# One of the two upper-half shuffles of the last but one pair of inverse outputs issued from SyncE's queue

## Chip, core and metric

The kernel runs on one core of one Trainium2 chip. The time is device microseconds of one execution, and the number that counts is the median of several executions. TensorE (PE) multiplies matrices, VectorE (DVE), ScalarE (ACT) and GpSimd (POOL) do the rest of the arithmetic, and SyncE (SP) computes nothing: it issues DMA transfers. GpSimd and ScalarE can issue transfers too.

## The reference

One layer of an H3-like state-space mixer is followed by a token-mixing MLP, in bf16, with S = 2048 positions and D = 448 channels:

```
h_q  = layernorm(x)                                  # x = A_q, over channels
kv   = shift_conv(k, shift_k, 4 taps) * v
y    = irfft(rfft(pad(kv)) * rfft(pad(ssm_k)))[:S]   # long causal convolution, per channel
h    = x + h_q * (y + kv * ssm_D)
u    = gelu(einsum("bsd,sf->bdf", layernorm(layernorm(h)), w1) + b1)     # F = 1792
out  = h + transpose(einsum("bdf,fs->bds", u, w2) + b2)
```

## The kernel before

The position axis is split as 128 partitions times R = 16 rows. The Fourier transforms are done as two matrix stages with a shuffle between them: `k1`, `k2` for the filter, `u1`, `u2` for `kv`, and back with `i1` and `i2`. A shuffle is a set of DMA transfers from SBUF to SBUF, since the second stage needs another index on the partitions than the first one leaves there.

The inverse transform is the place of the change. `emit_products_i1` (L1147 on) runs over eight pairs jj = 0 to 7. For each pair VectorE forms the products of the two spectra (L1161), TensorE multiplies them by the inverse tables (L1178), ScalarE evicts two PSUM pairs into the tile `TU` (the eviction helper, L739), and the two outputs j = 2jj and j = 2jj + 1 are then shuffled from `TU` into `TZ`. In every pair but jj = 7 each j has an upper transfer of 112 partitions (196 KB, issued by GpSimd) and a lower one of 16 partitions (28 KB, issued by SyncE), all at L1201. The upper transfer fills rows r = 0 to 13 of `TZ`, the lower one rows 14 and 15. The pair jj = 7 is done otherwise: its four transfers of 98 KB (L1190; three from SyncE, one from ScalarE) fill rows 2 to 15, and for rows 0 and 1 TensorE reads `TU` itself through small tables `EW`, which four small transfers of 4 KB (L1128, SyncE) prepare.

`emit_i2` then does the second inverse stage row by row. For r = 0 and 1 TensorE runs two matmuls on `TZ` (L1300) and four on `TU` (L1308); for the other rows only L1300. VectorE combines the result with the normalised input (L1337 for r = 0 to 3; for r from 4 on ScalarE or VectorE gates it first, L1317 or L1319, then L1327), takes statistics (L1343, L1346, with GpSimd's L1379 for the power) and writes the normalised row `Q` (L1386). The first MLP product (L1433) reads `Q` row by row; L1443 is its second half of columns, and L1455 the second MLP product, with L1458 adding the residual. All weights of the first product are loaded in four pieces (L1406; the second to fourth wait for the L1190 transfers), the rest later (L1410, L1417).

Each engine's order of work is written out by hand in `ORDER`, as tokens `step:operations`. The pair jj = 1, with j = 2 and 3, is the last but one that is worked on: TensorE takes the pairs as jj = 0, 6, 3, 4, 5, 2, 1, 7. Its step is `i1.4`: operations 18 and 20 are the upper transfers of j = 2 and 3, 19 and 21 the lower ones. `ct0.1:2-5` are the four L1128 transfers, `i1.6:22` a lower transfer of another pair, and `i1.16:22`, `i1.16:20`, `i1.16:19` the three L1190 transfers of SyncE. TensorE's order in `i2` is r = 0, 1, 4, 2, 7, 3, 6, 5, 8 and on; VectorE combines r = 0, 1, 2, 3 in this order.

A first pass in the program replays these orders with estimated costs, which fixes PSUM buffers and semaphores; the chip runs each engine's queue in the written order.

Of the kernel before, what the change touches and what calls it, by code (L numbers as in the profile page):

```python
# [78 lines left out]
    ),  # L79
# [8 lines left out]
    ),  # L88
}

# [493 lines left out]
def _build(nc, A_q, A_k, A_v, A_shift_k, A_ssm_k, A_ssm_D, B_w1, B_b1, B_w2, B_b2, out):  # L584
# [11 lines left out]
    DB = 2 * D  # L596
# [23 lines left out]
    o_TU = 104064  # L620
    o_KN = o_TU
    o_W2 = (o_TK, o_TU)
    o_TZ = 132736
# [15 lines left out]
    with ctx:  # L639
# [58 lines left out]
        def MR(s):  # L698
            return view(o_WR + s * 4 * DB, [4, D])
# [13 lines left out]
        def Pb(b, i=0):  # L713
            return PS[:, b.slots[i], 0:D]

        def Ppair(b):
            s0, s1 = b.slots
            return PS[:, s0:s1 + 1, 0:D]
# [15 lines left out]
        def evac(dst, src, w, b, n, scale=None, engs=FX, r=(), est=None):  # L734

            def fn(e, W):
                if W == "act":
                    if scale is None:
                        return e.copy(out=dst(), in_=src())  # L739
                    return e.activation(out=dst(), in_=src(), func=ACT.Copy, scale=scale)  # L740
                if scale is None:
                    return e.tensor_copy(out=dst(), in_=src())
                return e.tensor_scalar(out=dst(), in0=src(), scalar1=scale, scalar2=None, op0=ALU.mult)
            bs = [b] if b is not None else []
            return op(engs, fn, r=r, w=w, br=bs, n=n, kind="psum", est=est)
# [405 lines left out]
        def emit_products_i1():  # L1151
            for jj in range(R // 2):
                ms = []
                for h in range(2):
                    i = 2 * jj + h
                    sch.t0 = T_I1 + T_DI1 * i
                    m = _Buf(mring)
                    ms.append(m)
                    ru = (o_TU + i * 2 * DB, 2 * DB)
                    aft = [x for w in wbufs for x in w.readers] if i == 0 else [mfirst[0]]  # L1160
                    op("dve", lambda e, W, m=m, i=i: e.tensor_tensor(  # L1161
                        out=MR(m.slots[0]).rearrange("p (x y) d -> p x y d", x=2),
                        in0=TU[:, i].unsqueeze(2).broadcast_to([128, 2, 2, D]),
                        in1=TK[:, i].unsqueeze(1).broadcast_to([128, 2, 2, D]), op=ALU.mult),
                       r=[ru, (o_TK + i * 2 * DB, 2 * DB)], bw=[m], n=4 * D, after=aft)
                    if i == 0:
                        mfirst.append(len(sch.ops) - 1)
                bs = [_Buf(psum, 2) for _ in range(2)]
                if jj == 1:
                    sch.tag = "ct0"  # L1170
                    emit_ct(False)
                    sch.tag = "i1"
                mt = (MA, MB, MN) if jj < R // 2 - 1 else ML
                for h in range(2):
                    for t, (tab, xy) in enumerate(((mt[0], 0), (mt[2], 3), (mt[1], 1), (mt[1], 2))):
                        for par in range(2):
                            P = slice(64 * par, 64 * par + 64)
                            k = op("pe", lambda e, W, b=bs[h], m=ms[h], par=par, t=t, tab=tab, xy=xy, P=P: e.matmul(  # L1178
                                Pb(b, par), tab[P, :], MR(m.slots[0])[P, xy, :], start=(t == 0), stop=(t == 3)),
                               r=r_iv if jj < R // 2 - 1 else [(o_ML, 768)], br=[ms[h]], bw=[bs[h]], n=D, est=94.5, mode=3)  # L1180
                            i1_last.append(k)
                    evac(lambda jj=jj, h=h: TU[:, 2 * jj:2 * jj + 2, h, :], lambda b=bs[h]: Ppair(b),
                         [(o_TU + (4 * jj + h) * DB, DB), (o_TU + (4 * jj + 2 + h) * DB, DB)], bs[h], 2 * D)
                if jj == R // 2 - 1:
                    for h in range(2):
                        for par in range(2):
                            j = 2 * jj + par
                            p0 = 64 * (j & 1) + 32 * ((j >> 1) & 1) + (j >> 2)
                            o_h = o_TU + (2 * j + h) * DB
                            k = op("act" if h and par == 0 else "sp", lambda e, W, j=j, h=h, p0=p0: e.dma_start(  # L1190
                                TZ[p0:p0 + 29:4, NZ:R, h, :], TU[0:8 * (R - NZ), j, h, :]),
                                   r=[(o_h, DB)], w=[(o_TZ + NZ * 2 * DB, (14 - NZ) * 2 * DB, "zpool"), (o_TZ + 28 * DB, 4 * DB, "zsp")],
                                   dmab=8 * (R - NZ) * DB, keng=8)
                            shuf["zpool"] = k
                            shuf.setdefault("zl", []).append(k)
                    continue
                for par in range(2):
                    j = 2 * jj + par
                    p0 = 64 * (j & 1) + 32 * ((j >> 1) & 1) + (j >> 2)
                    for q_, a, b_, j0 in (("pool", 0, 112, 0), ("sp", 112, 128, 14)):  # L1200
                        shuf["z" + q_ + str(j)] = shuf["z" + q_] = op(q_, lambda e, W, j=j, p0=p0, a=a, b_=b_, j0=j0: e.dma_start(  # L1201
                            TZ[p0:p0 + 29:4, j0:j0 + (b_ - a) // 8].rearrange("p r c d -> p r (c d)"),
                            TU[a:b_, j].rearrange("p c d -> p (c d)")),
                           r=[(o_TU + j * 2 * DB, 2 * DB)], w=[(o_TZ + j0 * 2 * DB, (b_ - a) // 8 * 2 * DB, "z" + q_)],
                           dmab=(b_ - a) * 2 * DB, keng=8)

        def emit_warm(n_, t0):
# [219 lines left out]
        def emit_mlp():  # L1427
# [21 lines left out]
            for r in range(R):  # L1449
# [24 lines left out]
                ("u1", emit_stage1, (V, o_V, TU, o_TU, "u")),    # L1474
                ("xload", emit_xload, ()), ("bias", emit_bias, ()), ("q", emit_q, ()),
                ("u2", emit_stage2, (TU, o_TU, None)), ("ew", emit_ew, ()), ("i1", emit_products_i1, ()), ("ct", emit_ct, (True,)), ("xn", emit_xn, ()), ("w1a", emit_w1_load, (0,)),
                ("warm", emit_warm, (N_WZ, T_I2 - 50.0)),
                ("i2", emit_i2, ()), ("w1b", emit_w1_load, (1,)), ("w2", emit_w2_load, ()), ("mlp", emit_mlp, ()))
# [39 lines left out]
```

## Time and profile before

| what | value |
|---|---|
| median of 3 executions | 173.56 us (173.31 to 173.61) |
| the profiled execution | 173.39 us, its span 171.5 us |
| busy: PE, DVE, ACT, POOL | 162.2, 101.5, 92.6, 59.7 us |
| granted TensorE clock | full in all 40 slices |
| chain that ended last | PE 68%, ACT 18%, DMA 8%, DVE 3% |
| upper transfers of L1201 | 14 from GpSimd, 196 KB each, median 4.2 us from issue to landing |

Times in the views are us from the start of the span. The span leaves out 1.9 us of the execution's own time. A timeline row gives start, length, engine, line, operation and how many were merged, and in brackets the idle time before them with what ended it. A row of the chain gives start, length and what the end of the program was waiting for in that stretch. DMA-issuing instructions are shown on the queue of the engine that issues them (SPq is SyncE's, ACTq ScalarE's), with the time that the issue took, which is not the time of the transfer.

### The profile page before, as it was taken

What the parts mean: (1) busy time and instruction counts of PE and PEld (TensorE: products, weight loads), DVE (VectorE), ACT (ScalarE), POOL (GpSimd) and SP (SyncE); (2) the same over time, 40 slices, a digit from 0 to 9 for tenths busy, and PEclk for the clock granted to TensorE, in tenths of its full rate; (3) what the DMA queues carried; (4) which work ended last, traced back from release to release, by engine and by line L of the source; (5) the groups of instructions that cost most, each with busy time, mean ns of one, the idle gap of its engine ahead of it and who ended that gap; (6) DMA issues with size and microseconds to landing.
All of it is one profiled execution on the core that took longest, in us unless ns stands there. A gap on an engine that the chain in (4) does not pass through costs nothing.

```text
span 171.5 us, 3572 instructions
## 1 busy us (share of the span) xinstructions
PE 162.2 (95%) x1425; PEld 95.0 (55%) x1425; DVE 101.5 (59%) x188; ACT 92.6 (54%) x132; POOL 59.7 (35%) x152
## 2 busy tenths in 40 slices
PE   6999999889889999968999999999999999999994
PEld 2776745443334433543455555555567777777783
DVE  7997988869999999979999830000003133132231
ACT  3699688988999999969866536321210000000000
POOL 8344837581810686445887830000000000000000
PEclk9999999999999999999999999999999999999999
DMA  5999587584959756646899999990000111101111
GB/s 161 417 321 378 182 264 285 211 325 162 286 145 369 268 162 204 177 147 222 278 320 380 411 424 414 420 396 30 0 0 4 53 53 53 53 0 57 53 53 54
DMA packets 15628, 35.15 MB, mean 205 GB/s; under 512 B 3740, under 2 KB 9740, under 8 KB 15612
## 3 DMA queue, kind: packets, MB, share of 16 engines
q1 hardware_dynamic: 12468, 28.25, 45.5%
q0 software_dynamic: 2880, 6.49, 11.9%
q8 instruction: 11, 0.18, 0.4%
q10 hardware_dynamic: 264, 0.18, 0.3%
q14 instruction: 5, 0.04, 0.1%
HBM read 22.05 MB, written 1.84 MB: 139 GB/s over the span
## 4 chain that ended last, share of the span: by engine, by line
PE 68%; ACT 18%; DMA 8%; DVE 3%; issue 1%; POOL 1%; SPq 0%; DVEq 0%
PE ps L1455 25%; PE ps L1433 12%; PE ps L1443 12%; ACT arena L739 9%; DMA arena<-arena 8%; ACT arena L1070 5%; PE ps L1095 5%; PE ps L1178 4%; ACT arena L848 2%; PE ps L1060 2%; PE ps L1026 2%; PE ps L1300 2%; ACT arena L740 2%; PE ps L993 1%; DVE arena L1337 1%
## 5 line engine op out<-in xcount | busy, mean ns | idle before, releaser
L1458 DVE SCALAR_TENSOR_TENSOR arena<-ps,arena 128x448 bf16<-128x448 f32 (+2 forms) x17 | 11.1, 656 | 56.9 <-PE ps L1455 56.9
L1455 PE MATMUL ps<-arena 128*128 128x448 bf16 (+2 forms) x238 | 42.7, 342 | 0.0
L1455 PEld LDWEIGHTS ps<-arena 128*128 128x128 bf16 x238 | 33.3, 145 | 9.5
L739 ACT CAST arena<-ps 128x896 bf16<-128x896 f32 x30 | 24.6, 1012 | 0.2 <-PE ps L1095 0.2
L1433 PE MATMUL ps<-arena 128*128 128x448 bf16 x112 | 22.5, 353 | 0.7 <-DVE arena L1375 0.7
L1070 ACT CAST arena<-ps 128x896 bf16<-128x896 f32 x24 | 20.5, 919 | 3.2 <-PE ps L1060 3.2
L1076 POOL DMA_DIRECT2D arena<-arena x32 | 17.6, 556 | 11.8 <-ACT arena L1070 9.7
L1443 PE MATMUL ps<-arena 128*128 128x448 bf16 x112 | 21.4, 352 | 0.0
L1423 ACT ACTIVATE arena<-ps,arena 128x448 bf16<-128x448 f32 x14 | 8.3, 635 | 18.9 <-PE ps L1443 14.6
L1095 PE MATMUL ps<-arena 128*64 128x448 bf16 x128 | 15.2, 359 | 2.3 <-ACT arena L739 0.8
L1433 PEld LDWEIGHTS ps<-arena 128*128 128x128 bf16 x112 | 10.7, 98 | 11.4 <-DVE arena L1375 1.1
L1161 DVE TENSOR_TENSOR arena<-arena 128x1792 bf16<-128x1792 bf16 x16 | 16.7, 1086 | 0.3 <-ACT arena L739 0.2
L1443 PEld LDWEIGHTS ps<-arena 128*128 128x128 bf16 x112 | 11.0, 98 | 10.2
L1060 PE MATMUL ps<-arena 128*32 128x448 bf16 x256 | 14.9, 355 | 0.8 <-DVE arena L1008 0.5
L1178 PE MATMUL ps<-arena 64*128 64x448 bf16 x128 | 14.5, 351 | 0.1
L1201 POOL DMA_DIRECT2D arena<-arena x14 | 8.3, 599 | 13.7 <-ACT arena L739 13.7
L1095 PEld LDWEIGHTS ps<-arena 128*64 128x64 f16 x128 | 5.8, 108 | 10.7 <-ACT arena L739 2.9
L1178 PEld LDWEIGHTS ps<-arena 64*128 64x128 f16 x128 | 6.1, 94 | 8.2 <-ACT arena L739 2.5
L739 ACT COPY arena<-ps 128x1024 bf16<-128x1024 bf16 (+1 forms) x8 | 7.9, 1023 | 4.9 <-PE ps L967 3.5
L1008 DVE TENSOR_TENSOR arena<-ps,arena 128x512 bf16<-128x512 f32 (+1 forms) x16 | 9.1, 619 | 1.9 <-PE ps L993 1.7
L1355 ACT ACTIVATE arena<-arena 128x448 bf16<-128x448 f32 x14 | 8.0, 573 | 4.0 <-DVE arena L1327 3.8
L1060 PEld LDWEIGHTS ps<-arena 128*32 128x32 f16 x256 | 5.2, 95 | 7.5 <-DVE arena L1008 2.5
(96 smaller groups left out, 195.6 us busy)
## 6 DMA issues: line engine op xcount, KB each, us to landing
arena<-in_B_w_dram SPq DMA_DIRECT2D x8, 896.0 KB, 6.6
arena<-in_B_w_dram SPq DMA_DIRECT2D x2, 2048.0 KB, 18.0
arena<-arena POOLq DMA_DIRECT2D x32, 112.0 KB, 3.4
arena<-arena SPq DMA_DIRECT2D x16, 224.0 KB, 3.1
arena<-in_B_w_dram SPq DMA_DIRECT2D x2, 1536.0 KB, 19.5
arena<-arena POOLq DMA_DIRECT2D x14, 196.0 KB, 4.2
arena<-in_A_k_dram SPq DMA_DIRECT2D x4, 448.0 KB, 5.7
arena<-in_A_v_dram SPq DMA_DIRECT2D x4, 448.0 KB, 8.8
```

Of the source, the lines that this page charges most:

```text
L739: return e.copy(out=dst(), in_=src())
L1008: return e.tensor_tensor(out=v, in0=u.rearrange("p t (r d) -> p t r d", d=64), in1=v, op=ALU.mult)
L1060: op("pe", lambda e, W, b=b, r=r, q=q, x=x, c0=c0: e.matmul(PS[32 * q:32 * q + 32, b.slots[x], 0:D], E[:, 2 * r + x, c0:c0 + 32], src[:, r ...
L1070: return e.copy(out=dst, in_=Ppair(b)) if W == "act" else e.tensor_copy(out=dst, in_=Ppair(b))
L1076: shuf[tag].append(op(q_, lambda e, W, g=g, i=i, a=a, nu=nu, jh=jh: e.dma_start(T[a + i:a + i + 4 * nu - 3:4].rearrange("p (j k) c d -> p ...
L1095: op("pe", lambda e, W, b=bs[h], h=h, j=j, c=c, par=par: e.matmul(PS[64 * par:64 * par + 64, b.slots[c], 0:D], FW[:, 64 * c:64 * c + 64], ...
L1161: op("dve", lambda e, W, m=m, i=i: e.tensor_tensor(out=MR(m.slots[0]).rearrange("p (x y) d -> p x y d", x=2), in0=TU[:, i].unsqueeze(2).br ...
L1178: k = op("pe", lambda e, W, b=bs[h], m=ms[h], par=par, t=t, tab=tab, xy=xy, P=P: e.matmul(Pb(b, par), tab[P, :], MR(m.slots[0])[P, xy, :], ...
L1433: op("pe", lambda e, W, r=r, fc=fc, b=bs[fc]: e.matmul(Pb(b), W1A[:, r, 128 * fc:128 * fc + 128], Q[:, r, :], start=(r == 0), stop=(r == R ...
L1443: op("pe", lambda e, W, r=r, fc=fc, b=b: e.matmul(Pb(b), W1B[:, r, 128 * (fc - n0):128 * (fc - n0) + 128], Q[:, r, :], start=(r == 0), sto ...
L1455: op("pe", lambda e, W, r=r, fc=fc, b=b, d0=d0, d1=d1: e.matmul(Pb(b)[:, d0:d1], W2[fc // 7][:, fc % 7, r:S:R], G[:, fc, d0:d1], start=(fc ...
L1458: op("dve", lambda e, W, r=r, b=b, A=A, d0=d0, d1=d1: e.scalar_tensor_tensor(out=X[:, r, d0:d1], in0=Pb(b)[:, d0:d1], scalar=bm[:, r:r + 1 ...
```

## The change

The upper transfer of j = 3 (`i1.4:20`) leaves GpSimd's order and enters SyncE's, behind the four small transfers of L1128 and ahead of the three of L1190. Bytes, source, destination and the other transfers are the same. The third place of the diff keeps the name of the write group by the region that is written and not by the issuing engine, so that the order of the dependencies stays as it was.

```
 "pool": (
-  ... i1.6:21 i1.4:18 i1.4:20 q.4:4-5 q.2:4-5 xn.3:0 ...
+  ... i1.6:21 i1.4:18 q.4:4-5 q.2:4-5 xn.3:0 ...
 "sp": (
-  ... i1.6:22 ct0.1:5 ct0.1:2-4 i1.16:22 i1.16:20 i1.16:19 ...
+  ... i1.6:22 ct0.1:5 ct0.1:2-4 i1.4:20 i1.16:22 i1.16:20 i1.16:19 ...
...
-  for q_, a, b_, j0 in (("pool", 0, 112, 0), ("sp", 112, 128, 14)):
+  for q_, a, b_, j0 in (("sp" if j == 3 else "pool", 0, 112, 0), ("sp", 112, 128, 14)):
       shuf["z" + q_ + str(j)] = shuf["z" + q_] = op(q_, lambda e, W, ...: e.dma_start(
           TZ[p0:p0 + 29:4, j0:j0 + (b_ - a) // 8].rearrange("p r c d -> p r (c d)"),
           TU[a:b_, j].rearrange("p c d -> p (c d)")),
-         r=[(o_TU + j * 2 * DB, 2 * DB)], w=[(..., "z" + q_)],
+         r=[(o_TU + j * 2 * DB, 2 * DB)], w=[(..., "zsp" if j0 else "zpool")],
          dmab=(b_ - a) * 2 * DB, keng=8)
```

More of the change, by code (lines that the diff above doesn't have):

```diff
@@ L1203, in emit_products_i1 @@
                             TU[a:b_, j].rearrange("p c d -> p (c d)")),
-                           r=[(o_TU + j * 2 * DB, 2 * DB)], w=[(o_TZ + j0 * 2 * DB, (b_ - a) // 8 * 2 * DB, "z" + q_)],
+                           r=[(o_TU + j * 2 * DB, 2 * DB)], w=[(o_TZ + j0 * 2 * DB, (b_ - a) // 8 * 2 * DB, "zsp" if j0 else "zpool")],
                            dmab=(b_ - a) * 2 * DB, keng=8)
```

16 rows, old and new, of the table ORDER are left out of this document.

## Prediction

> **What bounds the kernel now.** I read the chain of waits first, because it says which event of the inverse transform the end hangs on. From 69 us it runs so:
>
> ```profile
> 69.09 1.13 ACT arena L739
> 70.22 0.28 issue
> 70.51 0.58 POOL arena L1201
> 71.09 4.36 DMA arena<-arena
> 75.45 0.05 issue
> 75.50 0.55 PE ps L1300 x2
> 76.05 0.77 PE ps L1308 x4
> 76.82 0.03 issue
> 76.84 0.68 DVE arena L1337
> ...
> 80.85 0.40 DVE arena L1386
> 81.25 0.07 DVE arena L1375
> 81.32 1.48 PE ps L1433 x7
> ...
> 94.79 10.59 PE ps L1433 x56
> 105.38 21.19 PE ps L1443 x112
> 126.57 42.08 PE ps L1455 x231
> ```
>
> ScalarE's last eviction of the pair ends at 70.22. GpSimd issues the upper transfer of j = 2 at 70.51 and that of j = 3 at 71.09, after 0.58 us of issuing. The second lands at 75.45, and only then does TensorE begin row r = 0. VectorE is released by that row at 76.84, writes the first row of Q, and from 81.32 TensorE is the chain to the end, with no gap of note. So whatever moves the 75.45 moves the end by as much, as long as nothing between 75.5 and 81.3 ends later for another reason.
>
> Next I looked at whether TensorE and VectorE really stand idle for it, at SP's queue around that time, and at how long each transfer of the pair took. These are the waits of the stretch, rows of the timeline, and the answers for L1201, first in the stretch that holds only the issue of j = 2, then for both of the pair, then over all fourteen:
>
> ```profile
> PE ps L1300 <- DMA arena<-arena: 1.5, 1, 1.5
> DVE arena L1337 <- PE ps L1308: 1.1, 1, 1.1
> ...
> 67.82 2.68 SPq L1128 DMA_DIRECT2D arena<-arena  x4
> 72.28 2.21 SPq L1190 DMA_DIRECT2D arena<-arena  x3
> 74.54 1.40 SPq L1201 DMA_DIRECT2D arena<-arena  x2
> 77.10 0.38 SPq L1406 DMA_DIRECT2D arena<-in_B_w_dram  x1
> ...
> DMA to landing us min/median/max: 3.0/3.0/3.0
> ...
> DMA to landing us min/median/max: 3.0/3.7/4.4
> ...
> DMA to landing us min/median/max: 2.9/4.2/6.3
> ```
>
> TensorE has nothing to do for 1.5 us and VectorE for 1.1. SP's queue is free from 70.50 (67.82 + 2.68) to 72.28. Of the pair, j = 2 landed 3.0 us after its issue (73.5), j = 3 4.4 after its own, 1.9 us behind j = 2 although it was issued only 0.58 behind it. The second one therefore pays for more than its place in the issue order: something in GpSimd's path or on the engines serves the two one after the other.
>
> **The change part by part.** *Removed from GpSimd:* one issue of 0.58 us. GpSimd's next work after the pair waits for VectorE, not for this issue, so that is worth nothing by itself:
>
> ```profile
> 72.14 0.24 POOL L1245 TENSOR_SCALAR arena<-arena 128x4 f32<-128x4 f32 x1 [0.46 <-DVE arena L1239]
> ```
>
> *Added to SP:* one issue. The price of an issue of that form on SP is that of L1190 or of SP's own L1201:
>
> ```profile
> L1190 SPq DMA_DIRECT2D arena<-arena x3: 668/691/697, 72.3 to 73.8; - x3
> L1201 SPq DMA_DIRECT2D arena<-arena x14: 666/667/706, 67.0 to 85.6; - x14
> SPq L1190 <- ACT arena L739: 1.8, 1, 1.8
> SPq L1406 <- DMA arena<-arena: 0.5, 1, 0.5
> ```
>
> That is 0.70 us, from 70.55 to 71.25. The wait that comes with it, for the eviction that ended by 70.22, is over before SP gets there. Behind it stand the three L1190 issues, which wait for another eviction until 72.28 (the 1.8 us of idle time above). So no issue on SP is later, and the cover that hides the 0.70 us is 1.0 us wide beyond it; without the cover L1190 would be issued up to 0.70 later.
>
> *Moved:* the transfer. Its issue goes from 71.09 to 70.55, and it no longer follows j = 2 in GpSimd's queue. What does it take from SP? The trace has no 196 KB transfer of SP. Nearest rows: the lone-looking transfer of j = 2, 3.0 us, is the lower bound. SP's 224 KB shuffles of the first stages give the spread when they share the DMA engines with GpSimd's:
>
> ```profile
> DMA to landing us min/median/max: 2.2/3.1/4.6
> 71.50:72.50 1.00, 1.00 (x13) 0.73 (x12) 0.97 (x4) 1.00 (x2) 0.45 (x3) 1.00 0.54 151
> 72.50:73.50 1.00, 1.00 (x17) 0.82 (x15) 0.96 (x5) 0.57 (x1) 1.00 (x1) 1.00 0.63 190
> 73.50:74.50 1.00, 0.49 (x7) 0.18 (x4) 0.96 (x3) 0.62 (x1) 0.92 (x3) 1.00 0.60 190
> 74.50:75.50 1.00, 0.00 (x1) 0.01 (x1) 1.00 (x3) 1.00 (x2) 0.23 (x2) 1.00 0.54 177
> ```
>
> The first row is the answer for L1076 on SP's queue (4.6 at worst). The others are stretches with the DMA engines' busy share and GB/s at the end: little more than half of them are busy, and they move 177 GB/s (the mean of 151, 190, 190 and 177). A transfer of 196 KB is 200.7 thousand bytes, so 1.13 us at that rate. If both transfers of the pair run on the same engines at the same time, the later one ends one transfer's data after the time of a lone one: 70.55 + 3.0 + 1.13, or 74.70 in round numbers. If they run on different engines, both land by 73.55. I take 74.70: the busy share near one half in all four stretches says that a transfer of this form does not spread over all sixteen engines, and I see nothing that would keep SP's off those of j = 2. The upper bound is the 6.3 us of the worst L1201 above, 76.85.
>
> A rule of the Trainium skill speaks against hoping for more: DMA: Bandwidth & Descriptors, section "Issuing engines are not separate DMA queues", says that a second issuing engine saves only the sequencer's issue time. By it the gain would be 0.54 us (71.09 less 70.55), close to the sum below, though the 1.9 us between the two landings is already more than the rule would have. The same page, section "Why a DMA increments its semaphore by 16 and not by 1", has SP's transfers always on the lowest-numbered engines and GpSimd's moving round, which would set the moved one on the engines of L1190; the busy share of 0.54 to 0.63 fits engines being used by halves, but no row names an engine.
>
> *What is late next.* Row 0 starts at 74.75 instead of 75.50. TensorE is free for it: its previous work ends at 74.0 (0.49 us busy in 73.5 to 74.5, then nothing). Rows 2 and up, in the order 4, 2, 7, 3, also need the four L1190 transfers, which SP saw landed at 77.10 (the 0.5 us wait of L1406):
>
> ```profile
> 77.83 2.81 PE L1300 MATMUL ps<-arena 128*128 128x448 bf16 x14
> 78.66 1.33 ACT L1317 ACTIVATE arena<-ps,arena 128x448 f32<-128x448 f32 x2
> 79.40 0.68 DVE L1337 SCALAR_TENSOR_TENSOR arena<-ps,arena 128x448 f32<-128x448 f32 x1
> 80.00 0.68 DVE L1337 SCALAR_TENSOR_TENSOR arena<-ps,arena 128x448 f32<-128x448 f32 x1
> ```
>
> Row 3 is the fourth pair of matmuls of the first of these rows, so it is ready 4 x 0.40 = 1.6 us after the first of them starts (14 in 2.81 us is 0.20 each), and VectorE takes it at 80.00. Hence the first may start as late as 78.35 for a gain of nothing, and in general the gain is at most 78.3 less the landing of L1190. With 77.10 that allows 1.2 us. L1190 now stands behind the moved transfer in SP's queue: four of 98 KB are 401 thousand bytes, 2.3 us at 177 GB/s, so behind a moved transfer that ends at 74.70 they are done at 77.0. I take 77.1 to 77.4, which leaves 0.9 us or more and does not cut the gain.
>
> *Sum.* 75.45 - 74.70 = 0.75 us off the start of row 0, of VectorE's chain and of the first L1433; everything behind is TensorE's own work. The profiled execution, 173.39 us for a span of 171.5, would become 172.64; it was 0.17 below the median of the runs, so against 173.56 I say 172.8.
>
> **The rivals.** *Absorbed (no change).* The moved transfer takes the engines ahead of L1190 by its full data, 1.13 us, and L1190 lands at 78.2 instead of 77.10. Then the gain is at most 78.3 - 78.2 = 0.1: 173.5. For it speaks that L1190 is issued only 1.7 us behind the moved transfer in the same queue; against it that the engines are only about half busy and that SP's three L1190 issues take 2.2 us, so that their transfers start one after the other and the first wait of them need not reach the last.
>
> *Slower.* SP's transfer is served behind GpSimd's transfer and lands late, at the price of the worst row of L1201, 6.3 us: 76.85. Place: between 70.55 and row 0. From a landing over 4.9 us after the issue (75.45) it costs time, and at 6.3 it costs 1.4 us: 175.0. For it: GpSimd's upper transfers show 2.9 to 6.3, so sharing can double one. Against it: the 6.3 comes from the stretch where they follow each other closely, while here only j = 2 is beside it; SP's 224 KB ones never took over 4.6.
>
> *More.* SP's transfer runs on other engines than j = 2, both land by 73.55, TensorE starts row 0 when it is free, at 74.05: 1.4 us, cut to 1.2 by L1190: 172.4. Against it: the half-busy engines.
>
> *Nothing done.* SP cannot issue it before 72.28, so that L1190 and it swap. The written order and the free 70.50 leave this little room; I count it with the absorbed case.
>
> **How the numbers follow.** A measurement of this kernel can tell about 0.2% (0.35 us) from no change. The forecast (gain 0.4 to 1.0) has 0.50, the larger gain 0.12, the absorbed case 0.20, the slower one 0.18. Faster is 0.50 + 0.12 = 0.62, the same 0.20, slower 0.18. The range goes from 172.3 (the larger gain with a little beyond) to 173.9: that holds the forecast, the absorbed case and the mild part of the slower one, and leaves out about 0.15 of slower cases and a few hundredths below. The forecast's own range is 172.5 to 173.2.
>
> **What would show it.** In the profile after, SP's queue has the moved L1201 at about 70.55 for 0.7 us and L1190 still at 72.28; the wait of L1300 for DMA shrinks from 1.5 us to about 0.8; row 0 starts near 74.75, the first L1433 near 80.6, and the chain still goes through that landing. L1406 still starts near 77.1 to 77.4. I am wrong if L1300 at r = 0 starts after 75.4 (the slower case), if a new wait of PE or VectorE for L1190's landing appears after row 1 (absorbed), or if row 0 starts at 74.1 (more).

## The result, and the profile after

| | before | after |
|---|---|---|
| median | 173.81 us (22 executions) | 173.03 us (22 executions, 172.07 to 174.32) |
| ratio, 95% interval | | 0.9957 [0.9939, 0.9976] |
| profiled execution, span | 173.39, 171.5 us | 173.40, 171.6 us |

The changed kernel is faster by 0.43%, which is 0.75 us of 173.81 (the medians differ by 0.78). The two profiled executions last the same, though: that of the changed kernel was 0.37 us above its own median, and its trace shows where that lies. These are rows of its timeline:

```profile
68.08 2.99 SPq L1128 DMA_DIRECT2D arena<-arena  x4
...
70.77 0.59 POOL L1201 DMA_DIRECT2D arena<-arena  x1 [2.07 <-ACT arena L739]
71.12 0.70 SPq L1201 DMA_DIRECT2D arena<-arena  x1
...
72.55 2.19 SPq L1190 DMA_DIRECT2D arena<-arena  x3
...
74.87 0.55 PE L1300 MATMUL ps<-arena 128*128 128x448 bf16 x2 [0.61 <-DMA arena<-arena]
...
77.75 0.38 SPq L1406 DMA_DIRECT2D arena<-in_B_w_dram  x1
...
77.78 2.82 PE L1300 MATMUL ps<-arena 128*128 128x448 bf16 x14 [0.41 <-DMA arena<-arena]
...
80.81 0.36 PE L1433 MATMUL ps<-arena 128*128 128x448 bf16 x1 [0.21 <-DVE arena L1375]
```

GpSimd issues one transfer, SyncE the other, at 71.12. Row 0 starts at 74.87 (75.50 before), the first L1433 at 80.81 (81.31). All of this execution was 0.27 us late when it came to the place of the change (the pair's eviction ended at 70.48, before at 70.21), so measured from that eviction row 0 is 0.89 us earlier and the first L1433 0.76. The waits of the stretch shrank as meant; TensorE's 1.5 us for the transfer are now 0.6, and a second, smaller wait for DMA has come in (0.41, above, for L1190):

```profile
PE ps L1300 <- DMA arena<-arena: 1.0, 2, 0.6
...
DVE arena L1337 <- PE ps L1308: 0.2, 1, 0.2
```

The chain of waits no longer goes through the moved transfer. It goes through the last L1190, and then through GpSimd at 86 to 90 us:

```profile
73.36 0.67 SPq L1190
...
74.07 3.66 DMA arena<-arena
...
77.78 1.70 PE ps L1300 x8
...
86.66 0.38 POOL arena L1370
...
87.13 0.57 POOL arena L1245
...
89.52 0.68 POOL arena L1379
...
90.23 0.94 DVE arena L1386 x2
...
105.42 21.19 PE ps L1443 x112
126.61 42.08 PE ps L1455 x231
```

Before, L1443 began at 105.38 and L1455 at 126.57, so from the eviction on only 0.22 us of the 0.89 reach L1455. 0.13 were gone at the first L1433, the rest between 85 and 92 us. These are waits of 82 to 93 us (us in total, times, longest), first of the kernel before and then of the changed one, and behind each its row of L1245:

```profile
ACT arena L1317 <- POOL arena L1248: 0.8, 1, 0.8
DVE arena L1386 <- POOL arena L1379: 0.6, 1, 0.6
```

```profile
87.33 0.26 POOL L1245 TENSOR_SCALAR arena<-arena 128x4 f32<-128x4 f32 x1
```

```profile
ACT arena L1317 <- POOL arena L1248: 1.3, 1, 1.3
DVE arena L1386 <- POOL arena L1379: 1.0, 1, 1.0
```

```profile
87.13 0.56 POOL L1245 TENSOR_SCALAR arena<-arena 128x4 f32<-128x4 f32 x1
```

VectorE and ScalarE waited longer for GpSimd's L1379 and L1248, and in front of both stands an L1245 that took twice as long. It accounts for little of the loss, though: from its start to that of L1379 it is 2.37 us, before 2.23, and the L1245 itself began only 0.47 us earlier after the eviction than before, so that most was lost ahead of it.

So the median gain has to be explained, and also why a single execution can keep little of it.

### The profile page after: what moved, and what is told of

Its sections match the earlier page's. It is cut to its first block, busy times and chain, and to the rows that moved or that the text cites. A ratio compares the mean times of both kernels' runs of the same rounds, so it can differ in the third digit from the quotient of the medians.

```text
span 171.6 us, 3572 instructions
## 1 busy us (share of the span) xinstructions
PE 162.0 (94%) x1425; PEld 94.4 (55%) x1425; DVE 101.4 (59%) x188; ACT 92.6 (54%) x132; POOL 59.5 (35%) x151
## 4 chain that ended last, share of the span: by engine, by line
PE 64%; ACT 15%; DMA 9%; DVE 5%; SPq 2%; POOL 2%; issue 2%; DVEq 0%; POOLq 0%
PE ps L1455 25%; PE ps L1443 12%; PE ps L1433 9%; ACT arena L739 8%; PE ps L1095 5%; DMA arena<-in_A_ssm_k_dram 5%; ACT arena L1070 4%; DMA arena<-arena 4%; PE ps L1178 4%; PE ps L1060 3%; PE ps L993 2%; PE ps L1300 2%; DVE arena L1008 2%; ACT arena L740 2%; SPq L888 1%
## 5 line engine op out<-in xcount | busy, mean ns | idle before, releaser
L1455 PE MATMUL ps<-arena 128*128 128x448 bf16 (+2 forms) x238 | 42.7, 342 | 0.0
L1455 PEld LDWEIGHTS ps<-arena 128*128 128x128 bf16 x238 | 33.3, 145 | 9.5
L1433 PE MATMUL ps<-arena 128*128 128x448 bf16 x112 | 22.6, 353 | 0.2 <-DVE arena L1375 0.2
L1076 POOL DMA_DIRECT2D arena<-arena x32 | 17.6, 556 | 13.1 <-ACT arena L1070 11.4
L1443 PE MATMUL ps<-arena 128*128 128x448 bf16 x112 | 21.4, 352 | 0.0
L1433 PEld LDWEIGHTS ps<-arena 128*128 128x128 bf16 x112 | 10.8, 98 | 10.9 <-DVE arena L1386 1.2
L1443 PEld LDWEIGHTS ps<-arena 128*128 128x128 bf16 x112 | 11.0, 98 | 10.2
L1201 POOL DMA_DIRECT2D arena<-arena x13 | 7.7, 599 | 13.7 <-ACT arena L739 13.7
L1386 DVE TENSOR_SCALAR arena<-arena 128x448 bf16<-128x448 f32 x16 | 7.7, 505 | 2.8 <-POOL arena L1379 2.8
```

The lines of the kernel that those rows point to most:

```text
L1076: shuf[tag].append(op(q_, lambda e, W, g=g, i=i, a=a, nu=nu, jh=jh: e.dma_start(T[a + i:a + i + 4 * nu - 3:4].rearrange("p (j k) c d -> p ...
L1433: op("pe", lambda e, W, r=r, fc=fc, b=bs[fc]: e.matmul(Pb(b), W1A[:, r, 128 * fc:128 * fc + 128], Q[:, r, :], start=(r == 0), stop=(r == R ...
L1443: op("pe", lambda e, W, r=r, fc=fc, b=b: e.matmul(Pb(b), W1B[:, r, 128 * (fc - n0):128 * (fc - n0) + 128], Q[:, r, :], start=(r == 0), sto ...
L1455: op("pe", lambda e, W, r=r, fc=fc, b=b, d0=d0, d1=d1: e.matmul(Pb(b)[:, d0:d1], W2[fc // 7][:, fc % 7, r:S:R], G[:, fc, d0:d1], start=(fc ...
```

## The experiments

Times "after the eviction" count from the end of ScalarE's last eviction of the pair (70.21 before), so that executions that came there earlier or later can be compared. Two theories stood at the start. One: two queues serve the pair side by side, where GpSimd's alone serves its two one after the other. The other: what matters is only that SyncE's path is the quicker one for a transfer. Both leave open which DMA engines are used.

### The changed kernel again (e_after, e_after2)

No edit; twice more against the kernel before.

> The changed kernel itself, taken again so that its parts and the other variants have a profile and times from the same chip. Theory A (the end follows the later landing of the last pair, and row 0 starts 0.6 to 0.9 us earlier relative to the work before it): 0.4% under the kernel before, 0.3 to 0.6%. Rival B (the gain of the first comparison is drift between runs): within 0.2%.

> The changed kernel once more, for the size of its gain: the first comparison gave 0.43% and the second 0.15%, and in the two profiles row 0 started 4.39 and 5.10 us after the eviction, with the moved issue 0.64 and 1.07 us after it. Theory F (the gain varies from execution to execution with when SyncE comes free): 0.2 to 0.4% under before, with single times that spread more than those of the kernel before. Rival B (no gain): within 0.1%.

Measured: 173.2 us, 0.9985 [0.9958, 1.0012], and 173.02 us, 0.9963 [0.9937, 0.9988]. The three comparisons together put the gain at 0.3 to 0.4%, with the middle one, taken alone, not to be told from no change. Their profiles show a spread that the prediction did not have. These are the answer for SyncE's L1128 (min/median/max ns of an issue) and rows of the timeline in e_after:

```profile
L1128 SPq DMA_DIRECT2D arena<-arena x4: 624/651/1373, 68.6 to 71.4; - x4
```

```profile
72.06 0.70 SPq L1201 DMA_DIRECT2D arena<-arena  x1
...
76.08 0.55 PE L1300 MATMUL ps<-arena 128*128 128x448 bf16 x2 [1.32 <-DMA arena<-arena]
...
93.57 0.54 PE L1300 MATMUL ps<-arena 128*128 128x448 bf16 x2 [0.47 <-DMA arena<-arena]
```

And in e_after2 the same answer, and the chain's row of the moved transfer (start is its issue, length its time to landing):

```profile
L1128 SPq DMA_DIRECT2D arena<-arena x4: 624/651/1227, 67.7 to 70.4; - x4
```

```profile
71.02 4.19 DMA arena<-arena
```

One of the four small issues ahead of the moved one took 1.37 or 1.23 us in place of 0.65, so that SyncE came to the moved transfer 1.07 and 0.93 us after the eviction, and it landed at 5.05 and 5.12 (5.24 before). In those two executions row 0 gained 0.1 to 0.2 us. The median of the second comparison gained 0.64 us all the same, so one profile does not stand for the executions behind its median. In the first profile of the changed kernel the longest was 0.93 us, the issue came at 0.64 and the landing at 4.34. Why an issue stalls is open.

### Both uppers of the pair from SyncE (e_both)

```
 "pool": -  ... i1.4:18 q.4:4-5 ...      +  ... q.4:4-5 ...
 "sp":   -  ... ct0.1:2-4 i1.4:20 ...    +  ... ct0.1:2-4 i1.4:18 i1.4:20 ...
-  ("sp" if j == 3 else "pool", 0, 112, 0)
+  ("sp" if j in (2, 3) else "pool", 0, 112, 0)
```

> Both upper transfers of the last pair from SyncE (j = 2 ahead of j = 3), none from GpSimd. Theory A (what made j = 3 late is GpSimd's own slow service of two transfers in a row; from SyncE both run on one set of engines either way): SyncE issues at 70.5 and 71.2, the later lands near 74.8, time as the changed kernel, 0.7 us under before. Rival C (the gain is that two queues issue in parallel): the two follow each other again, the later lands at 75.3 to 75.8 and the time is that of the kernel before within 0.2 us.

Measured: 173.63 us, 0.9989 [0.9967, 1.0012]: no gain. The chain of this kernel, from the second issue on:

```profile
71.16 0.48 SPq L1201
71.68 4.03 DMA arena<-arena
...
75.75 0.55 PE ps L1300 x2
```

The first of the two landed 3.72 us after the eviction, the second 5.19, which is where the second one landed before. So SyncE's queue is not the quicker path; by the transfer records (the trace's entries for the pieces that the DMA engines move) seven to nine pieces are in work at a time while its two move, and they land 1.47 us apart. This run does not show that the gain comes of a second queue beside GpSimd's: the second issue here came 1.16 us after the eviction, and with an issue as late as that one queue each gains nothing either (e_dose, below).

### Which DMA engines the two use (e_flip, e_flip_before, e_par, e_alone, e_free, e_free_par)

A small GpSimd transfer of 2 KB, far ahead of the pair, was meant to shift the engines that GpSimd's later transfers use; in the changed kernel (e_flip) and in the kernel before (e_flip_before):

```
 "pool": -  ... ew.0:2 i1.14:19 ...      +  ... ew.0:2 ew.0:4 i1.14:19 ...
+  op("pool", lambda e, W: e.dma_start(FL[0:8, :], ID[0:8, :]), ...)
```

> The changed kernel with one extra tiny transfer (8 partitions, 2 KB, into a scratch place) issued by GpSimd ahead of the inverse shuffles, where GpSimd is idle. If GpSimd's transfers alternate between two sets of engines, this puts j = 2 on the set that SyncE's transfers do not use. Theory A (SyncE's moved transfer and j = 2 share their engines, and that is why it took 3.7 us): the moved one lands after 3.0 us, row 0 starts 0.5 us earlier than in the changed kernel (it is then held by TensorE's earlier work), L1190 lands 0.4 us earlier, time 0.3 to 0.6 us under the changed kernel, about 172.5. Rival D (the 3.7 us is SyncE's own price, with no sharing): as the changed kernel within 0.2 us.

> The kernel before with the same extra tiny transfer: the control. The last pair swaps its engine sets, j = 3 then shares with L1190. Theory A: row 0 as before within 0.2 us or earlier if the 0.7 us by which the last engine trailed belongs to one set of engines; L1190 lands up to 0.6 us later with no cost, time within 0.3 us of before. Rival D: nothing changes but the extra issue, which is hidden, within 0.2 us.

Measured: e_flip 173.2 us, 0.9971 [0.9951, 0.9991]; e_flip_before 173.37 us, 0.9996 [0.9968, 1.0024]. It shifted nothing: the transfer records of e_flip, counted in steps of 0.2 us, show eight to nine pieces in work at a time while GpSimd's transfer hands over to SyncE's, as in the changed kernel. Its profile is the cleanest of the changed order, with no long issue ahead (L1128's row, and the chain):

```profile
L1128 SPq DMA_DIRECT2D arena<-arena x4: 624/627/676, 68.1 to 70.2; - x4
```

```profile
70.87 4.05 DMA arena<-arena
...
126.04 42.08 PE ps L1455 x231
```

Issue 0.33 us after the eviction, landing 4.38, L1455 0.86 us earlier from the eviction than before: the whole of row 0's gain arrives.

To have j = 3 on other engines than j = 2, one transfer of the same form was taken out of GpSimd's sequence ahead of it: the first upper transfer of all, j = 12, went to SyncE as well (e_par).

```
 "pool": -  ... i1.14:19 i1.14:21 ...    +  ... i1.14:21 ...
 "sp":   -  ... xload.1:0 i1.6:22 ...    +  ... xload.1:0 i1.14:19 i1.6:22 ...
-  "sp" if j == 3                        +  "sp" if j in (3, 12)
```

> The changed kernel with the first upper transfer of all (j = 12) given to SyncE too, so that every later transfer of GpSimd takes the other place in its alternation. Theory A (GpSimd's transfers alternate between two halves of the DMA engines, SyncE's use one of them): j = 2 now runs on the other half than before, and the moved one lands about 3.0 us after its issue, row 0 4.0 us after the eviction. Theory E without halves (any transfer of GpSimd in flight holds SyncE's): landing 3.7 to 4.0 us after its issue as in the changed kernel.

In e_alone the upper transfer of j = 2 reads the output of j = 0 and is issued long before, so that nothing runs beside j = 3; those rows of `TZ` hold another output's values.

```
 "pool": -  ... i1.14:21 i1.8:19 ... i1.4:18 q.4:4-5 ...   +  ... i1.14:21 i1.4:18 i1.8:19 ... q.4:4-5 ...
-  TU[a:b_, j]                           +  TU[a:b_, 0 if j == 2 and a == 0 else j]
```

> The upper transfer of j = 2 reads j = 0's output instead of its own, so that GpSimd can issue it early, among the first pairs; SyncE's moved transfer of j = 3 is then alone at the end. What is computed for j = 2's rows is another output. Theory E (SyncE's transfer waits on the DMA engines until GpSimd's transfer of j = 2 has moved its data): the moved one lands 2.9 to 3.1 us after its issue instead of 3.7 to 4.05, row 0 starts when TensorE's earlier work ends, 3.8 to 4.0 us after the eviction, L1190 lands 0.3 to 0.5 us earlier than in the changed kernel. Rival D (3.7 to 4 us is SyncE's own price for this transfer): it lands 3.7 to 4.0 us after its issue all the same and row 0 starts no earlier than in the changed kernel.

In e_free SyncE is freed ahead of the pair: a lower transfer of another pair goes behind L1190. In e_free_par that and the edit of e_par are both made.

```
 "sp":   -  ... i1.6:22 ct0.1:5 ct0.1:2-4 i1.4:20 i1.16:22 i1.16:20 i1.16:19 i1.1:20 ...
         +  ... ct0.1:5 ct0.1:2-4 i1.4:20 i1.16:22 i1.16:20 i1.16:19 i1.6:22 i1.1:20 ...
```

> The changed kernel with one lower transfer (j = 5, rows 14 and 15) moved in SyncE's order from ahead of the four L1128 transfers to behind L1190, so that SyncE has issued L1128 long before the eviction and is free when it ends. Theory F (a good part of the gain hangs on when SyncE comes free: the moved issue came 0.33 to 1.07 us after the eviction): the moved issue comes 0.1 us after the eviction in every execution, row 0 starts 0.2 to 0.7 us earlier than in the profiles of the changed kernel, time 0.6 to 1.0 us under the kernel before. Theory E alone (the moved transfer waits for j = 2's data whenever it is issued): row 0 starts 4.4 us after the eviction as in the best profile so far, time 0.7 us under before, with less spread. Rival (SyncE's queue was never the limit): as the changed kernel within 0.2 us.

> SyncE free when the eviction ends (the lower transfer of j = 5 behind L1190, as in the run before) and the first upper transfer of all given to SyncE, so that j = 2 runs on the other half of the DMA engines. Theory G (with both on one half, early issue by SyncE only makes the two interleave and land together at 4.6 to 4.8; on two halves each goes at its own pace): moved issue 0.03 us after the eviction, landing 3.1 to 3.8, j = 2 at 3.3 to 3.9, row 0 at 3.9 to 4.0 where TensorE's earlier work ends; time 1.0 to 1.3 us under before, 172.4. Rival (two transfers at once slow each other on whatever engines): row 0 at 4.4 or later, time 0.6 to 0.8 us under before at best.

Measured: e_par 175.6 us and e_alone 172.34 us, one execution each (e_par's was 2.9 us late long before the place of the change, so only its distances count); e_free 173.2 us, 0.9994 [0.9971, 1.0017]; e_free_par 172.83 us, 0.9954 [0.9929, 0.9979]. The chain's row of the moved transfer in e_par, in e_free and in e_free_par, and then row 0 and the rows behind it in e_alone's timeline:

```profile
73.44 4.26 DMA arena<-arena
```

```profile
70.89 4.79 DMA arena<-arena
```

```profile
70.15 4.48 DMA arena<-arena
```

```profile
74.07 0.54 PE L1300 MATMUL ps<-arena 128*128 128x448 bf16 x2
...
77.06 2.82 PE L1300 MATMUL ps<-arena 128*128 128x448 bf16 x14 [0.50 <-DMA arena<-arena]
```

Three things follow. First, sharing is real. Alone, the moved transfer landed 3.08 us after its issue (3.74 after the eviction); beside j = 2 it took 3.70 and 4.05 in the changed kernel and e_flip, 4.79 in e_free, where it was issued 0.27 us ahead of GpSimd's and both landed together, at 4.63 and 4.82. So on the same engines a still earlier issue is no better: the data of the two were mixed, and e_free took the time of the kernel before. Second, they shared one half of the engines: pieces in work at a time come to eight or nine in the changed kernel, e_flip and e_free, and to fifteen in e_par and e_free_par. This agrees with the Trainium skill, DMA: Bandwidth & Descriptors, section "Why a DMA increments its semaphore by 16 and not by 1": SyncE's transfers take the lowest-numbered engines, GpSimd's a group that moves round; here one GpSimd transfer less put the two on different halves. Why e_flip's small transfer did not is open. Third, different halves help little: the landings are 4.57 and 4.50 after the eviction, 0.1 to 0.2 later than in the best executions of the plain change. The trace shows a landing as several signals, here called parts: in e_par seven parts came between 76.76 and 76.99 and the last at 77.70, in e_free_par the last came 0.99 us behind the one ahead of it. One late part took the gain.

The kernel before has such a late part too, and neither theory has it. By its transfer records j = 2 and j = 3 were already on different halves there and overlapped: j = 3's data began 2.45 us after the eviction, those of j = 2 ended at 2.97, and up to fifteen pieces were in work. Of j = 3's landing fifteen of sixteen parts had come by 4.52, and the last came at 5.24, 0.72 later; in the control e_flip_before it was 0.41 (4.64 and 5.05). So it is with the second upper transfer of every pair of the kernel before: its last part came 0.27 to 1.71 us behind the fifteenth, in the first of each pair 0.01 to 0.14. In the changed kernel the moved transfer's data began at 2.67, later than that, as those of j = 2 ended on the same engines, and no part was late (the last two at 4.33 and 4.34). So of the 0.90 us between the two landings 0.72 are one late part. What makes a part late is open, and no run has j = 3 from GpSimd without one, so that it is not settled how much of the gain is owed to the other queue.

In e_alone TensorE no longer waited for row 0 at all, and L1190 then held it for 0.50 us at 77.06: about 1.4 us is the most that this place can give to row 0, and the end gets less (1.0 us at L1455).

### When SyncE comes to it (e_late, e_dose)

e_late puts the moved transfer behind the three L1190 of SyncE:

```
 "sp":   -  ... ct0.1:2-4 i1.4:20 i1.16:22 i1.16:20 i1.16:19 ...
         +  ... ct0.1:2-4 i1.16:22 i1.16:20 i1.16:19 i1.4:20 ...
```

> The moved transfer placed behind the three L1190 issues in SyncE's queue instead of ahead of them. Theory A (its landing sets the start of row 0 and that sets the end, one for one): issue 4.3 us after the eviction, landing near 7.3, row 0 2.0 us later than in the kernel before; time 1.8 to 2.1 us over before, 175.5. Rival (there is other slack behind row 0 that takes part of it up): under 1.2 us over before.

Measured: 179.28 us, 1.0342 [1.0304, 1.038], 5.7 us over the kernel before (173.54 in this comparison); far more than expected. Row 0 explains 3.56 us of it: it starts 8.84 us after the eviction, 5.28 before (2.0 later was expected, but behind L1190 the moved transfer took 4.47 us to land). The rest is the clock. The wait of row 0, then slices of 2 us (PE, PEld, DVE, ACT, POOL busy, granted clock, DMA share, GB/s), then the group of L1308 at 80 to 84 us here, and last that at 75 to 81 in the kernel before:

```profile
PE ps L1300 <- DMA arena<-arena: 5.1, 1, 5.1
```

```profile
78.00:80.00 2.00, 0.00 (x0) 0.00 (x0) 0.00 (x0) 0.00 (x0) 0.00 (x0) 0.61 0.59 139
80.00:82.00 2.00, 1.80 (x5) 0.74 (x6) 0.00 (x0) 0.00 (x0) 0.00 (x0) 0.50 0.92 314
82.00:84.00 2.00, 2.00 (x7) 0.87 (x6) 1.34 (x3) 0.87 (x1) 0.40 (x2) 0.50 0.87 255
84.00:86.00 2.00, 2.00 (x9) 0.94 (x8) 1.00 (x4) 1.21 (x3) 0.88 (x1) 0.68 1.01 355
```

```profile
L1308 PE MATMUL ps<-arena 128*128 128x448 bf16 x6 | 2.7, 581 | 0.0
```

```profile
L1308 PE MATMUL ps<-arena 128*128 128x448 bf16 x8 | 1.8, 352 | 0.0
```

TensorE idled for 5.1 us, and its clock fell to half before it had work again. The first L1433 starts 5.77 us later than before (16.87 against 11.10 after the eviction), 2.2 us more than row 0.

e_dose delays the moved issue by one other issue of SyncE only, with L1190 where it was:

```
 "sp":   -  ... ct0.1:2-4 i1.4:20 i1.16:22 i1.16:20 i1.16:19 i1.1:20 i1.1:22 ...
         +  ... ct0.1:2-4 i1.1:20 i1.4:20 i1.16:22 i1.16:20 i1.16:19 i1.1:22 ...
```

> The changed kernel, with the lower transfer of j=0 (another transfer of SyncE's, that nothing near waits for) put ahead of the moved one in SyncE's order, so that the moved one is issued some 0.7 us later, 1.0 to 1.8 us after the end of the pair's eviction. Theory (the moment at which SyncE comes to the moved transfer sets the gain: issues at 0.33 and 0.64 us after the eviction landed at 4.38 and 4.34, issues at 0.93 and 1.07 at 5.12 and 5.05, the kernel before at 5.24): landing 5.1 to 5.8 us after the eviction, row 0 between 0.1 us earlier and 0.5 us later than in the kernel before, the time within 0.2 per cent of the kernel before or up to 0.3 per cent above it. Rival (the gain comes of GpSimd being rid of one transfer, whenever SyncE issues it): as the changed kernel, 0.3 to 0.4 per cent under the kernel before.

Measured: 173.89 us, 1.001 [0.9986, 1.0034]: the gain is gone. The chain:

```profile
71.49 4.05 DMA arena<-arena
...
75.59 0.55 PE ps L1300 x2
```

Issued 1.05 us after the eviction it landed at 5.10, row 0 began at 5.14 (5.28 before). This is what the stalled issues of e_after and e_after2 did by chance, now done on purpose, and it came out as the theory written down for it said: GpSimd being rid of a transfer is worth nothing unless SyncE is there in time. At row 0 an issue at 0.64 us still gained in full, one at 0.93 hardly.

It is not the delay of the issue itself that is lost. By the transfer records the moved data begin at the same time in the changed kernel's three profiles, e_flip, e_pool and e_dose, 2.65 to 2.72 us after the eviction, as those of j = 2 end. Issued by 0.64 they then took 1.3 to 1.5 us; issued at 0.93 to 1.07 they took 2.1 (in e_dose with the pieces of the small transfer ahead counted in). In e_after and e_after2 they went slower from the start (half were done at 3.64 and 3.72, against 3.34 in the first profile), and 28 and 27 pieces of L1190 had begun before nine tenths of the moved ones were done, against 4. So L1190, which does not move with the moved issue, shares the engines when SyncE is late. That this is the cause is argued: no run moves L1190 alone.

### GpSimd's part behind the change (e_pool)

The wait for L1379 that ate the gain in the first profile was taken away by giving L1379 its place ahead of L1248:

```
 "pool": -  ... i2.50:0 q.8:5 i2.51:0 ...    +  ... i2.50:0 i2.51:0 q.8:5 ...
```

> The changed kernel with two neighbours in GpSimd's order swapped: the power for the pair r = 8 and 9 (L1379) ahead of that for the input rows 12 to 15 (L1248). Theory H (in the changed kernel's profile the chain between 85 and 92 us ran through GpSimd's L1248, VectorE waited 1.0 us for L1379 there, and about 0.5 us of the gain at the first L1433 was lost by L1443): the wait goes, 0.2 to 0.5 us under the changed kernel, 172.7. Rival (ScalarE's gate behind L1248, 0.7 us later now, takes its place): as the changed kernel within 0.2 us.

Measured: 173.43 us, 0.9976 [0.9949, 1.0003]: not better than the changed kernel. The waits at 82 to 93 us show why: that wait is gone, and ScalarE's for L1248, 1.3 us in the changed kernel (above), is now 2.0, with VectorE waiting behind it.

```profile
ACT arena L1317 <- POOL arena L1248: 2.0, 1, 2.0
DVE arena L1319 <- PE ps L1300: 1.4, 1, 1.4
```

## Why the prediction was right, and where it was right by luck

It said 172.8 us, 0.75 us under the median it started from; the changed kernel took 173.03, by the ratio 0.75 under the median beside it, and inside the range. That the two gains agree to the hundredth is luck: the repeats gave 0.26 and 0.64 us. Point by point, from one profile of each kernel, all us after the eviction:

| kernel | moved issue | landing of the later upper | last L1190 landed | row 0 | L1455 less row 0 | ratio |
|---|---|---|---|---|---|---|
| before | (GpSimd 0.87) | 5.24 | 6.87 | 5.28 | 50.91 | |
| after | 0.64 | 4.34 | 7.25 | 4.39 | 51.57 | 0.9957 |
| e_after | 1.07 | 5.05 | 7.61 | 5.10 | 51.53 | 0.9985 |
| e_after2 | 0.93 | 5.12 | 7.25 | 5.16 | 50.91 | 0.9963 |
| e_flip | 0.33 | 4.38 | 6.89 | 4.43 | 50.91 | 0.9971 |
| e_flip_before | (GpSimd 0.87) | 5.05 | 6.84 | 5.09 | 50.91 | 0.9996 |
| e_both | 1.16 | 5.19 | 7.72 | 5.23 | 50.91 | 0.9989 |
| e_free | 0.03 | 4.82 | 6.88 | 4.91 | 50.90 | 0.9994 |
| e_free_par | 0.03 | 4.50 | 7.11 | 4.55 | 50.91 | 0.9954 |
| e_dose | 1.05 | 5.10 | 7.29 | 5.14 | 50.92 | 1.0010 |
| e_pool | 0.32 | 4.47 | 7.18 | 4.52 | 51.60 | 0.9976 |

**Row 0 sets the end, one for one.** Right in most executions: from row 0 to the first L1455 it is 50.90 to 50.92 us in eight of these eleven, whatever row 0 did. In the other three 0.6 to 0.7 us were lost behind it. In the first profile it was the GpSimd stretch above; in e_after TensorE waited 0.47 us at 93.57 for a transfer that landed late (row above); e_pool has its own edit there, and the long L1245 as well. "Everything behind is TensorE's own work" was therefore too strong. That the longer L1245 is the cause in the first profile is only argued; e_alone's profile has it too, and all three executions with it (0.56 us each) have a wait of TensorE for L1190 ahead of it (0.41, 0.21 and 0.50 us in the changed kernel, e_pool and e_alone); no run here separates the two.

**Why j = 3 was late before.** Wrong. The prediction read the 1.9 us between the two landings as two transfers served one after the other. They overlapped on different halves of the engines, and 0.72 us of the 1.9 are one late part. The forecast did not rest on this reading, since 74.70 was added up from the time of a lone transfer. But it is luck that the moved transfer has no such part: in e_par and e_free_par it has one, of 0.70 and 0.99 us.

**When SyncE issues.** The prediction read 70.50 as the moment at which SyncE is free and took 70.55, 0.33 after the eviction. e_flip and e_pool have just that (0.33, 0.32). But the 70.50 came from one execution, and a long L1128 moved it to 0.64, 0.93 and 1.07 in the three profiles of the changed kernel itself. This is the term that was mis-sized most: e_dose shows that 0.7 us here is the whole gain.

**How long the transfer takes.** 3.0 + 1.13 = 4.13 us was taken, for two transfers on the same engines. Measured: 3.08 alone (e_alone), 4.05 when issued at 0.33 (e_flip), so 0.97 for the other's data; 3.70 when issued at 0.64. In the first profile the later issue (0.31 us more than taken) and the shorter transfer (0.43 less) cancelled, and the landing, predicted 4.48 after the eviction (74.70 less 70.22), was 4.34. Reading the half-busy engines as shared halves was right.

**The rule against it.** The Trainium skill, DMA: Bandwidth & Descriptors, section "Issuing engines are not separate DMA queues", allows only the issue time. The trace differs: in the first profile the issue moved 0.23 us (0.87 to 0.64), the landing 0.90. That the engines are shared, which the same section says, the runs bear out. The difference is not shown to be the second queue's doing: the moved data began later than j = 3's did before (2.67 us after the eviction against 2.45), and the part ahead of the late one came at 4.52, only 0.18 behind the moved transfer's landing. With both in one queue of SyncE the gain was zero, but there the second issue was late as well.

**Absorbed by L1190.** In part. It landed at 7.25 after the eviction, 0.38 later than before, where 0.0 to 0.3 was said. By the prediction's own bound (78.3, here 78.57, less 77.73) the gain is at most 0.84, and 0.76 reached the first L1433. "Does not cut the gain" was off by 0.1 us there. The bound itself is 0.05 us too small by the prediction's own numbers (80.00 less 1.6 is 78.4, not 78.35). And two of the signs that the prediction named speak for this case: the chain left the moved transfer for the last L1190, and TensorE has a new wait for L1190, 0.41 us, which was to show that the forecast is wrong. So part of the absorbed case is in the first profile, beside the forecast's own signs (the wait of row 0 at 0.61 us, where about 0.8 was said).

**More.** Wrong as a time: on different engines the pair did not land by 3.3 after the eviction but at 4.50 and 4.57. **Slower:** no moved issue took the 4.9 us after which it would cost time, 4.79 in e_free being the most. It took e_late's order to be slower, by another mechanism. **Nothing done** fell with the first row of the timeline.

No version beats the changed kernel for certain: e_free_par, with 0.9954, has the same ratio to within its interval.

## What to carry to other kernels

When two transfers that one row waits for leave one issuing queue together, giving the later one to another queue can bring its landing forward by more than the issue time, even where both end on the same DMA engines: here 0.90 us for 0.23. But look at how the later landing ends before calling it a matter of queues, since 0.72 of these 0.90 us were one late part. Before counting on it, see in several executions when that other queue comes free, since here 0.7 us decided between the whole gain and none. And work out what lands next: the room ends where the following transfer or the next engine's chain takes over.

## What the runs showed of the hardware that was not expected

A short stall at the wrong place costs twice. After 5.1 us without work TensorE's granted clock was 0.50 until past 84 us, a matmul took 581 ns in place of 352, and 3.56 us of delay at row 0 became 5.8 at L1455 (61.97 against 56.19 after the eviction). The Trainium skill, TensorE: Matmul & The Clock Gate, section "What's actually happening", has the clock at half after about 3.4 us of idleness, and the trace agrees: idle from 75.1, a mean of 0.61 in 78 to 80 means half clock from about 78.4. It has the full clock back after about 3.4 us of work; here, by the 0.68 of 84 to 86, it was about 5 us after work began at 80.19. The 1.5 us wait of the kernel before stayed under that, and the clock was full behind it.

SyncE's issues of the same small transfer, 0.62 to 0.68 us as a rule, took up to 0.93, 1.23 and 1.37 us in the three profiles of the changed kernel, and up to 1.10, 0.96 and 0.86 in e_free_par, e_alone and e_late; in the kernel before, e_flip, e_pool and e_dose none took over 0.68.
